# Convolution, spectral mixing and a gated output on one NeuronCore: unit borders, early transposes and the order around the last mixing

## Chip, cores and metric

One core of one Trainium2 chip runs the kernel; seven idle. The metric is the device time of one execution in microseconds (us), lower is better. Engines: TensorE (PE; its weight loads are shown as PEld), VectorE (DVE), ScalarE (ACT), GpSimd (POOL) and SyncE (SP). TensorE writes its results into PSUM, which has eight banks; DVE and ACT take them from there. POOL's queue issues all loads but one, SP's queue issues all stores.

## What is computed

x has shape (8, 3264, 192): batch, sequence, channels, float32. First a causal convolution of 7 taps along the sequence, one softmaxed set of taps for each of 8 heads of 24 channels. Its output u goes through a Fourier transform along the sequence of which the first 64 modes are kept; each mode has its own complex 192x192 matrix; the inverse transform y is added and a gated term follows.

```python
w = softmax(weight)                                # (8 heads, 7 taps)
x = einsum('hk,bskhg->bshg', w, x_unfolded)        # convolution
X = rfft(x, axis=1)[:, :64]
Y = X * (w_r + 1j * w_i)                           # per mode a 192x192 product
u = x + irfft(Y, n=S, axis=1)
return u + maximum(u @ w_ch, 0)
```

## The kernel before, in words

The order of all work is written out by hand: the program's order is each engine's order, and semaphores are set from what each instruction reads and writes.

**Layout.** Batches are taken in four pairs, q = 0 to 3. The sequence of a pair is cut into NB = 13 blocks of 256 positions; a block lies on 128 partitions with two positions each, so a pair has NT = 26 tiles of 128 rows by 2 batches by 192 channels. xall holds all 52 blocks in bf16; the convolution reads its input there and writes its result into the slots one block before. ct holds the transposed rows of all tiles, 312 pieces of 128x128; its last 108 pieces first hold weight groups 5 to 10. arena holds tables at first, then weight groups, at last the output buffers. The 64 modes are 16 groups of four (g); two DMAs bring a group (real and imaginary half), and group g+11 goes where group g was, once mixing g has read it.

**Convolution** (conv_pieces, conv_step; L286 to L345). The work is cut into units, each a run of n blocks of one pair: 5 and 8 blocks for pair 0, 7 and 6 for each of the others. A unit has 8 heads of two steps; a step is four matmuls of the lower 64 rows and, two steps later, four of the upper 64, into one PSUM bank (L297, 64x64 array tiles, 48 n columns). After a head, DVE and ACT copy its results to xall (L334 to L344). While a unit's loads (load_unit, L147, on POOL's queue) have not landed, its matmuls wait. At the head of the program L184 runs 85 idle matmuls, and L434 a few more behind unit 0.

**Transform** (dft, L352): per tile one matmul with ftab, the table of cosines and sines, all tiles of a pair summed in one bank in two or three runs; xtrans (L366) transposes the sums into xt, the input of the mixing. Both are put between heads of the next unit (loop at L438).

**Transposes** (c_bank, L400): eight tiles' pieces are transposed into a bank (L398) and copied to ct by DVE or ACT in turn (two to one). 39 such banks are needed before the output. One is done ahead of the last transform run (L470), the others stand in the list tjobs (L501) behind four banks that transpose ftab and one that makes wsw from w_ch (w_bank).

**Mixing** (L650 to L692). For each pair of groups: mix (L515) twice, ACT's copy of the result (mix_copy, L527), three jobs of tjobs, mix_trans (transposes of the mixed modes, copied to yet by DVE and ACT), three more jobs. The last groups are interleaved with the first output pieces (both, L569) and zw_pair (L594): the mixed modes times w_ch and times the identity, for pairs 1 to 3, into zwl; mixings 14 and 15 are not in these, and their modes enter later as "late rows": late_rows (L529) computes them for all batches and POOL issues 16 small DMAs into zwl. For pair 0, zw is computed after mixing 15 (L686 to L692).

**Output** (L700 to L776). A tile's result is c (transposed rows times w_ch, from ct), plus g (ftab times zw's w_ch half), clamped at zero by ACT (L640), plus y (ftab times zw's other half), then DVE adds u (L629) and SP stores two tiles at a time. Tiles 0 to 3 are begun by hand; the other 100 ("items") go through a ring of eight PSUM banks, with the two row halves of different items side by side (L716). Item 0's c, and the g of tiles 0 to 3, stand right behind zw (L748 to L755).

Of the kernel before, what the change touches and what calls it, by code (L numbers as in the profile page):

```python
# [20 lines left out]
def kernel(  # L21
# [25 lines left out]
    MAGIC = 12582912.0  # L47
    NIDLE = 85
    UNITS0 = ((0, 5), (5, 8))
    UNITS = ((0, 7), (7, 6))  # L50
    units = [(q, b0, n) for q in range(NQ) for b0, n in (UNITS if q else UNITS0)]

# [93 lines left out]

    def load_unit(q, b0, n):  # L147
        nf = min(n, NB - 1 - b0)
        s0 = NB * q + b0 + 1
        for i in range(2):  # L150
            off = ((2 * q + i) * S + 2 * P * b0) * D
            src = bass.AP(tensor=x.tensor, offset=x.offset + off, ap=[[2 * D, P], [2 * P * D, nf], [1, 2 * D]])
            nc.gpsimd.dma_start(out=xin[:, s0:s0 + nf, 2 * D * i:2 * D * (i + 1)], in_=src)  # L153
        if nf < n:
            off = (2 * q * S + 2 * P * (NB - 1)) * D
            src = bass.AP(tensor=x.tensor, offset=x.offset + off, ap=[[2 * D, PL], [S * D, 2], [1, 2 * D]])
            nc.gpsimd.dma_start(out=xin[0:PL, s0 + nf, :].rearrange("p (i c) -> p i c", i=2), in_=src)  # L157
# [106 lines left out]
    for k, u in enumerate(units[4:]):  # L264
        load_unit(*u)
        if k == 1:
            nc.gpsimd.dma_start(out=wm[:, 0:D], in_=moe_w_ch[0:P, :])
        if k == 2:
            nc.gpsimd.dma_start(out=w1[64:P, 0:D], in_=moe_w_ch[P:D, :])
# [16 lines left out]
    def conv_pieces(step, row):  # L286

        (q, b0, n, h, a), z, _ = step
        s0 = NB * q + b0 + 1
        r = slice(64 * row, 64 * row + 64)  # L290
# [13 lines left out]
    def conv_step(u):  # L304
# [3 lines left out]
        if u is not None:  # L308
            if u[0]:
                z = free.pop(0)  # L310
            else:
                z = flow[-2][0][2] if u[4] else free.pop(0)
            flow[-1] = [(u, z[:, u[4] if u[0] == 0 else 0, :], z), []]
            lower = conv_pieces(flow[-1][0], 0)
# [6 lines left out]
        if old is not None:  # L321
            turn(old[1][2:])
            for _ in upper:
                pass
        if old is None or old[0][0][4] == 0:
            return
        (q, b0, n, h, _), _, tile1 = old[0]
        s0 = NT * q + 2 * b0
        dst = xall[:, s0:s0 + 2 * n, :, GRP * h:GRP * h + GRP].rearrange("p (b a) i e -> p a b i e", a=2)
        tile0 = flow[-2 - CONVLAG][0][2]  # L330
        if q == 0:
            srcv = tile0[:, :, 0:2 * GRP * n].rearrange("p a (b i e) -> p a b i e", b=n, i=2)
            if h in ((0, 1, 2, 3, 4, 6) if b0 == 0 else (0, 1, 3, 5)):
                nc.scalar.copy(out=dst, in_=srcv)  # L334
            else:
                nc.vector.tensor_copy(out=dst, in_=srcv)  # L336
# [14 lines left out]

    def dft(q, t0, t1):  # L352

        z = free.pop(0)
        xp = z[:, 0, 0:2 * D]
        for t in range(t0, t1):
            k = PL if t >= NT - 2 else P
            nc.tensor.matmul(xp, ftab[0:k, t, :], xall[0:k, NT * q + t, :, :],  # L358
                             start=(t == t0), stop=(t == t1 - 1), skip_group_check=True)
        if t0 == 0:  # L360
            nc.scalar.copy(out=xacc, in_=xp)
        else:
            nc.vector.tensor_tensor(out=xs[q % 2][:, :, :].rearrange("p i d -> p (i d)"), in0=xp, in1=xacc, op=ALU.add)
        free.append(z)
# [56 lines left out]
    for step in range(4):  # L421
        table(step, *PA)
    chores = {(0, 0): [(PB, (0,))], (0, 5): [(PA, (4,))], (0, H): [(PA, (5,)), (PB, (1, 2, 3)), (PC, range(4))],
              (1, H): [(PC, (4, 5))]}

# [5 lines left out]
    def idle(n):  # L431
# [4 lines left out]
        free.append(z)  # L436

    for k, u in enumerate(units):  # L438
        for h in range(H):
            for a in range(2):  # L440
                conv_step((*u, h, a))
            tables(k, h)
            if k > 1 and h == (4 if k == 2 else 2):
                if pend:
                    xtrans(pend.pop(0))
                dfts()
        if k == 2:
            for g in range(NW + NL):
                load_w(g)
        if u[0]:  # L450
            todo.append((u[0], 2 * u[1], 2 * (u[1] + u[2])))
            continue
# [3 lines left out]
        if k == 0:  # L456
            idle(4)
            dft(0, *PA)
            for step in (4, 5):
                table(step, *PB)  # L460
            idle(3)
        else:

            ones = open_psum("left", (1, 1, 1, 1)) + open_psum("right", (1, 1, 1, 1))
            free[:] = [ones[2 * twos.index(z) + i] for z in free for i in range(2)]
            todo.append((0, PA[1], NT))
    flush()

    z = free.pop(0)
    c_bank(8, z[:, 0, :].bitcast(BF16))  # L470
    free.append(z)
    dfts()
# [28 lines left out]
    tjobs = [(g_bank, 8 * k, min(8, NT - 8 * k)) for k in range((NT + 7) // 8)] + [(w_bank,)]  # L501
    tjobs += [(c_bank, k) for k in range(0, 3 * NT * NQ, 8) if k != 8]

    def some(n):
        for _ in range(n):
            if tjobs:
                f, *a = tjobs.pop(0)
                f(*a)

    def mix(g, bank):  # L510
        yp = bank[:, D * (g % 2):D * (g % 2) + D]
        for j in range(3):
            for p4 in range(4):
                m = 4 * g + p4
                nc.tensor.matmul(yp[32 * p4:32 * p4 + 2 * B, :], xt[:, j, :, m],  # L515
                                 wts[g][:, p4, j, :], start=(j == 0), stop=(j == 2),
                                 tile_position=(0, 32 * p4), skip_group_check=True)
        load_w(g + NW + NL)

# [8 lines left out]

    def late_rows(bank):  # L529

        m0 = MODES - 8
        for t in range(2):
            nc.tensor.matmul(bank[:, 0:2 * D], yet[:, t, 2 * B * m0:2 * B * MODES], (wm, w1)[t][:, :], start=(t == 0), stop=(t == 1),
                             skip_group_check=True)
        nc.scalar.copy(out=ylate, in_=bank[:, 0:2 * D])  # L535
        for m in range(8):
# [4 lines left out]

    def mix_trans(d, g0, n):
        et = [z.bitcast(BF16)[:, 0:n * P].rearrange("p (g k) -> p g k", g=n) for z in ze]
        for t in range(2):
            for g in range(n):
                trans(et[t][:, g, :], ymix[:, 2 * d + g0 + g, 64 * t:64 * t + P])
        m0 = 8 * d + 4 * g0
        for t in range(2):
            dst = yet[:, t, 2 * B * m0:2 * B * (m0 + 4 * n)].rearrange("p (m k) -> p m k", k=2 * B)
# [44 lines left out]
    def zw_pair(q, bw, by):  # L594

        for t, bank in enumerate((bw, by)):
            for i in range(2):
                zw_mm(2 * q + i, bank[:, D * i:D * i + D], t)
        for t, bank in enumerate((bw, by)):
            dst, srcv = zwl[:, 2 * q - 2:2 * q, t, :], bank[:, 0:2 * D].rearrange("p (b d) -> p b d", b=2)  # L600
            if t == 0:
                nc.scalar.copy(out=dst, in_=srcv)
# [46 lines left out]

    some(2)  # L650
    xtrans(NQ - 1, ze)
    some(2)
    ND = NG // 2

    for d in range(ND - 2):
        mix(2 * d, zm[d % 2])
        mix(2 * d + 1, zm[d % 2])
        mix_copy(d, zm[d % 2], 0, 2)
        some(3)
        mix_trans(d, 0, 2)  # L660
        some(3)
    d = ND - 2
    mix(2 * d, zm[0])
    some(99)
    mix(2 * d + 1, zm[0])
    mix_copy(d, zm[0], 0, 2)
    sl = [z[:, 0, :] for z in open_psum("left", (1, 1, 1, 1))]
    place[0] = sl[0:2]
    both(0, 0, "c", begin=True)
    mix_trans(d, 0, 2)  # L670
    both(0, 1, "c")
    zw_pair(1, ze[0], ze[1])
    zw_pair(2, sl[2], sl[3])
    d = ND - 1
    mix(NG - 2, zm[1])
    mix_copy(d, zm[1], 0, 1)
    zw_pair(3, zm[0], sl[2])
    mix_trans(d, 0, 1)
    mix(NG - 1, zm[1])
    mix_copy(d, zm[1], 1, 1)  # L680

    place[1], ze = ze, sl[2:4]
    both(1, 0, "c", begin=True)
    mix_trans(d, 1, 1)
    both(1, 1, "c")
    for b in range(2):  # L686
        zw_mm(b, zm[b][:, 0:D], 0)
    for b in range(2):
        zw_mm(b, ze[1][:, D * b:D * b + D], 1)
    nc.vector.tensor_copy(out=zw[:, 0, 0, :], in_=zm[0][:, 0:D])  # L690
    nc.scalar.copy(out=zw[:, 0, 1, :], in_=zm[1][:, 0:D])
    nc.vector.tensor_copy(out=zw[:, 1, 0:2, :].rearrange("p b d -> p (b d)"), in_=ze[1][:, 0:2 * D])  # L692

    def whole(n, which):
        for a in range(2):
            full(n, which, a)


# [4 lines left out]
    K = len(items)  # L703
    ring = ze + zm[1:2] + place[0] + place[1] + zm[0:1]
    taken = [0]
# [19 lines left out]
    def take(k):  # L725
        bank[k] = next_of_ring()
        place.setdefault(items[k][0], []).append(bank[k])

    def upper_y(k):
        if 0 <= k < K - 2:  # L730
# [17 lines left out]
    for k in range(LAG):  # L748
        take(k)
        for j, p in enumerate(pieces(k, 0, "c")):  # L750
            product(k, 0, p, j == 0, False)
        whole(k, "g")
        clamp(place[k][0], False)
        clamp(place[k][1])
    late_rows(zm[0])  # L755
    for k in range(K + 4):
# [52 lines left out]
```

## Time and profile before

| | us |
|---|---|
| median of three runs | 172.9 (172.82 to 173.41) |
| the profiled execution | 173.26 |
| its span, first to last instruction | 171.5 |
| TensorE busy | 161.1 (94%) |
| DVE / ACT / POOL busy | 128.3 / 113.7 / 51.8 |
| convolution, L297 | 9.5 to 69 |
| mixings 0 to 15, L515 | 74.7 to 103.1 |
| output loop, L716 without a gap | 108.9 to 165.7 |

The granted TensorE clock was 0.997 on average. The page has a row for each engine with its busy tenths in 40 slices of 4.3 us, and one for the 16 DMA engines; the chain of waits goes back from the last instruction to what released each step; the list of waits gives for each pair of engines and lines the total, the number and the longest. In the timeline a row is start, duration, engine, line, operation, and in brackets the idle time before it with what ended it. Four steps of the order below (L297, L358, L398, L515) are the convolution, the transform, the transposes and the mixing.

### The profile page before, as it was taken

What the parts mean: (1) busy time and instruction counts of PE and PEld (TensorE: products, weight loads), DVE (VectorE), ACT (ScalarE), POOL (GpSimd) and SP (SyncE); (2) the same over time, 40 slices, a digit from 0 to 9 for tenths busy, and PEclk for the clock granted to TensorE, in tenths of its full rate; (3) what the DMA queues carried; (4) which work ended last, traced back from release to release, by engine and by line L of the source; (5) the groups of instructions that cost most, each with busy time, mean ns of one, the idle gap of its engine ahead of it and who ended that gap; (6) DMA issues with size and microseconds to landing.
All of it is one profiled execution on the core that took longest, in us unless ns stands there. A gap on an engine that the chain in (4) does not pass through costs nothing.

```text
span 171.5 us, 6925 instructions
## 1 busy us (share of the span) xinstructions
PE 161.1 (94%) x2897; PEld 134.8 (79%) x2897; DVE 128.3 (75%) x262; ACT 113.7 (66%) x226; POOL 51.8 (30%) x93
## 2 busy tenths in 40 slices
PE   6998989999998999979999999999999999999980
PEld 6984867877867687669999875699898989898950
DVE  4899964637747384567776846799998999999990
ACT  8485874546546274277777664688888888888870
POOL 7998432424322453444432000790000000000000
PEclk9999999999999999999999999999999999999998
DMA  2999999999999999999999950489999989999995
GB/s 30 202 203 204 204 208 198 204 203 202 205 202 205 210 204 207 207 206 207 206 206 207 206 90 4 147 303 351 340 330 344 345 320 352 345 333 336 334 360 193
DMA packets 37151, 40.14 MB, mean 234 GB/s; under 512 B 2464, under 2 KB 37120, under 8 KB 37120
## 3 DMA queue, kind: packets, MB, share of 16 engines
q0 software_dynamic: 22816, 19.62, 71.4%
q1 hardware_dynamic: 14304, 20.09, 31.9%
q8 instruction: 22, 0.36, 0.8%
q14 instruction: 9, 0.07, 0.1%
HBM read 39.10 MB, written 20.05 MB: 345 GB/s over the span
## 4 chain that ended last, share of the span: by engine, by line
PE 80%; DMA 10%; POOL 3%; ACT 2%; issue 1%; DVE 0%; POOLq 0%; ACTq 0%; DVEq 0%
PE z L716 34%; PE z L297 16%; PE z L398 12%; DMA xall<-in_x_dram 10%; PE z L358 10%; PE z L515 3%; POOL xall L153 3%; PE z L647 1%; PE z L591 1%; PE z L375 1%; PE z L592 1%; PE z L582 1%; ACT ftab L393 1%; ACT z L479 1%; POOL xall L157 0%
## 5 line engine op out<-in xcount | busy, mean ns | idle before, releaser
L629 DVE TENSOR_TENSOR arena<-z,xall 128x384 f32<-128x384 f32 (+1 forms) x103 | 56.4, 557 | 3.4 <-PE z L716 1.5
L640 ACT ACTIVATE z<-z 128x384 f32<-128x384 f32 x102 | 48.5, 475 | 12.2 <-PE z L716 2.4
L716 PEld LDWEIGHTS <-ct 64*128 64x128 bf16 x600 | 42.3, 94 | 3.7 <-PE z L647 0.6
L716 PE MATMUL z<-arena,ftab 64*128 64x384 bf16 x308 | 44.9, 322 | 0.0
L297 PE MATMUL z<-xall,shared 64*64 64x336 bf16 (+3 forms) x1024 | 38.6, 294 | 1.8 <-DMA xall<-in_x_dram 1.0
L297 PEld LDWEIGHTS <-shared 64*64 64x64 bf16 x1024 | 33.2, 106 | 7.4 <-issue 4.9
L716 PE MATMUL z<-wsw,ct 64*128 64x192 bf16 x300 | 35.1, 243 | 0.0
L344 DVE CAST xall<-z 128x336 bf16<-128x336 f32 (+1 forms) x48 | 22.9, 483 | 12.5 <-PE z L297 10.2
L716 PEld LDWEIGHTS <-ftab 64*128 64x128 bf16 x396 | 29.7, 93 | 2.7 <-issue 0.5
L342 ACT CAST xall<-z 128x336 bf16<-128x336 f32 (+1 forms) x48 | 20.1, 418 | 15.4 <-PE z L297 11.3
L716 PE MATMUL z<-wm,ct 64*128 64x192 bf16 x200 | 29.9, 243 | 0.0
L716 PE MATMUL z<-w,ct 64*128 64x192 bf16 x100 | 24.3, 243 | 0.0
L395 DVE COPY ct<-z 128x1024 bf16<-128x1024 bf16 x27 | 17.4, 686 | 5.5 <-PE z L398 2.4
L398 PE MATMUL z<-ident,xall 128*128 128x128 bf16 x312 | 19.8, 219 | 0.0
L358 PE MATMUL z<-xall,ftab 128*128 128x384 bf16 (+1 forms) x104 | 18.3, 327 | 0.7 <-DVE xall L336 0.7
L398 PEld LDWEIGHTS <-xall 128*128 128x128 bf16 x312 | 17.8, 98 | 1.0 <-issue 0.2
L153 POOL DMA_DIRECT2D xall<-in_x_dram x16 | 14.7, 930 | 9.9 <-DMA xall<-in_x_dram 9.1
L358 PEld LDWEIGHTS <-ftab 128*128 128x128 bf16 (+1 forms) x104 | 9.6, 98 | 8.0 <-issue 1.2
L716 PE MATMUL z<-mixa,ftab 64*128 64x384 bf16 x88 | 13.6, 323 | 0.0
L393 ACT COPY ct<-z 128x1024 bf16<-128x1024 bf16 x12 | 12.1, 1012 | 2.1 <-PE z L398 1.9
L539 POOL DMA_DIRECT2D arena<-xs x16 | 7.9, 504 | 16.6 <-ACT xs L535 16.6
L184 PE MATMUL z<-xall 128*128 128x144 bf16 x85 | 7.9, 276 | 1.6 <-DVE xall L171 1.6
(113 smaller groups left out, 155.0 us busy)
## 6 DMA issues: line engine op xcount, KB each, us to landing
out_dram<-arena SPq DMA_DIRECT2D x47, 384.0 KB, 3.4
xall<-in_x_dram POOLq DMA_DIRECT2D x8, 672.0 KB, 16.8
xall<-in_x_dram POOLq DMA_DIRECT2D x8, 480.0 KB, 16.8
arena<-in_moe_w_r_dram POOLq DMA_DIRECT2D x10, 288.0 KB, 11.1
arena<-in_moe_w_i_dram POOLq DMA_DIRECT2D x10, 288.0 KB, 11.2
ct<-in_moe_w_r_dram POOLq DMA_DIRECT2D x6, 288.0 KB, 11.4
ct<-in_moe_w_i_dram POOLq DMA_DIRECT2D x6, 288.0 KB, 11.5
out_dram<-arena SPq DMA_DIRECT2D x4, 288.0 KB, 3.2
```

Source lines behind the costliest of these rows:

```text
L153: nc.gpsimd.dma_start(out=xin[:, s0:s0 + nf, 2 * D * i:2 * D * (i + 1)], in_=src)
L184: nc.tensor.matmul(free[3][:, 0, 0:144], zeros[:, 0:P], zeros[:, 0:144], start=True, stop=True, skip_group_check=True)
L297: yield nc.tensor.matmul(o, band[r, h, int(a != a1), c0:c0 + 64], xin5[r, s1:s1 + n, :, a1, dsl], start=(row == 0 and a1 == 0), stop=(row ...
L342: nc.scalar.copy(out=dst[:, a], in_=srcv)
L344: nc.vector.tensor_copy(out=dst[:, a], in_=srcv)
L358: nc.tensor.matmul(xp, ftab[0:k, t, :], xall[0:k, NT * q + t, :, :], start=(t == t0), stop=(t == t1 - 1), skip_group_check=True)
L393: nc.scalar.copy(out=out, in_=in_)
L395: nc.vector.tensor_copy(out=out, in_=in_)
L398: nc.tensor.matmul(o, in_, ident[:], start=True, stop=True, is_transpose=True)
L629: nc.vector.tensor_tensor(out=o[0:pn, :, a, :], in0=srcv, in1=xall[0:pn, s + a, :, :], op=ALU.add)
L640: nc.scalar.activation(out=z, in_=z, func=ACT.Relu)
L716: mm = nc.tensor.matmul(target(bank[k], cols, r), l, r, start=first, stop=last, skip_group_check=True)
```

## The change

- Units are counted over all 52 blocks: 5, 8, 9, 10, 10, 10, so that three of them cross from one pair to the next (parts_of splits them for the loads and the transform). Six units instead of eight, 768 convolution matmuls instead of 1024.
- Pair 0's remaining transform (tiles 6 to 25) stands right behind unit 1 instead of inside unit 2; for its first ten tiles heads 0 to 5 come first, heads 6 and 7 after.
- Four banks of transposes (fill) stand ahead of unit 3, two ahead of unit 4; the one ahead of the last transform stays. The last banks of ct, where weights lie, are held back until those are mixed (clear). Behind the last transform, xtrans is followed by four jobs instead of two.
- c of ring item 0 moves ahead of mixing 15; the ring's banks get another order.
- late_rows is split: its matmuls (late_mm) stand ahead of the g of tiles 0 to 3, its copy and DMAs stay.
- One reader to a bank: zw of pair 0 goes into two banks, one copied by ACT, one by DVE (before: three); the last mix_trans uses one bank and one DVE copy; zw_pair computes 384 columns per batch in one bank instead of 192 columns four times in two.
- The sine table's step 4 of the last third moves from behind unit 1 to its head 5; the moe_w_ch loads move by one unit; idle matmuls 92 instead of 85 at the start, three fewer behind unit 0.

```diff
-    NIDLE = 85
-    UNITS0 = ((0, 5), (5, 8))
-    UNITS = ((0, 7), (7, 6))
-    units = [(q, b0, n) for q in range(NQ) for b0, n in (UNITS if q else UNITS0)]
+    NIDLE = 92
+    UNITS = (5, 8, 9, 10, 10, 10)
+    units = [(sum(UNITS[:k]), n) for k, n in enumerate(UNITS)]
...
+    def parts_of(g0, n):
+        while n > 0:
+            q, b0 = divmod(g0, NB)
+            m = min(n, NB - b0)
+            yield q, b0, m
+            g0, n = g0 + m, n - m
...
-    def dft(q, t0, t1):
+    def dft(q, t0, t1, early=0):
...
+        DE = 6 * GRP
+        work = [(t, slice(0, DE)) for t in range(t0, t0 + early)] + [(t, slice(DE, D)) for t in range(t0, t0 + early)]
+        work += [(t, slice(0, D)) for t in range(t0 + early, t1)]
...
+    def fill(n):
+        for _ in range(n):
+            z = free.pop(0)
+            c_bank(8 * next(early_banks), z[:, 0, :].bitcast(BF16))
+            free.append(z)
+    early_banks = iter(range(1, 9))
     for k, u in enumerate(units):
+        fill({3: 4, 4: 2}.get(k, 0))
...
-            if k > 1 and h == (4 if k == 2 else 2):
-                if pend:
+            if k > 1 and h in (2, 6):
+                if pend and (k, h) != (2, 2):
                     xtrans(pend.pop(0))
-                dfts()
+                if h == 2:
+                    dfts()
...
-            idle(3)
...
-            todo.append((0, PA[1], NT))
+            dft(0, PA[1], NT, 10)
+            pend.append(0)
...
-    tjobs += [(c_bank, k) for k in range(0, 3 * NT * NQ, 8) if k != 8]
+    tjobs += [(c_bank, k) for k in range(0, 3 * NT * NQ, 8) if not 8 <= k < 64]
+    def clear(f, a):
+        last = a[0] + 7 - (3 * NT * NQ - NL * WGB // P) if f is c_bank else -1
+        return last < 0 or NW + last // (WGB // P) < mixed[0]
...
     some(2)
     xtrans(NQ - 1, ze)
-    some(2)
+    some(4)
...
+    ring = [sl[3], zm[0], sl[2]] + sl[0:2] + ze + zm[1:2]
...
     mix_trans(d, 0, 1)
+    take(0)
+    lower_c(0)
     mix(NG - 1, zm[1])
     mix_copy(d, zm[1], 1, 1)
-    place[1], ze = ze, sl[2:4]
+    place[1] = ze
     both(1, 0, "c", begin=True)
-    mix_trans(d, 1, 1)
+    mix_trans(d, 1, 1, sl[2])
     both(1, 1, "c")
     for b in range(2):
-        zw_mm(b, zm[b][:, 0:D], 0)
+        zw_mm(b, zm[0][:, D * b:D * b + D], 0)
     for b in range(2):
-        zw_mm(b, ze[1][:, D * b:D * b + D], 1)
-    nc.vector.tensor_copy(out=zw[:, 0, 0, :], in_=zm[0][:, 0:D])
-    nc.scalar.copy(out=zw[:, 0, 1, :], in_=zm[1][:, 0:D])
-    nc.vector.tensor_copy(out=zw[:, 1, 0:2, :].rearrange("p b d -> p (b d)"), in_=ze[1][:, 0:2 * D])
+        zw_mm(b, sl[2][:, D * b:D * b + D], 1)
+    late_mm(zm[1])
+    nc.scalar.copy(out=zw[:, 0, 0:2, :].rearrange("p b d -> p (b d)"), in_=zm[0][:, 0:2 * D])
+    nc.vector.tensor_copy(out=zw[:, 1, 0:2, :].rearrange("p b d -> p (b d)"), in_=sl[2][:, 0:2 * D])
```

## The prediction

> **What bounds the kernel now.** I read the page first: busy shares and the 40 slices.
>
> ```profile
> PE 161.1 (94%) x2897; PEld 134.8 (79%) x2897; DVE 128.3 (75%) x262; ACT 113.7 (66%) x226; POOL 51.8 (30%) x93
> ...
> PE   6998989999998999979999999999999999999980
> ...
> DMA  2999999999999999999999950489999989999995
> ```
>
> Two things are full at once. TensorE is full from slice 6 on; the DMA engines are full from slice 1 to 22 (4 to 99 us) with loads alone, then empty for 9 us. So until about 100 us TensorE and the load stream run side by side, and only the later of them counts. The chain of waits in order of time shows which one the profile followed:
>
> ```profile
> 24.48 3.04 PE z L297 x72
> ...
> 68.96 0.55 PE z L398 x8
> ...
> 69.52 2.14 PE z L358 x12
> ...
> 102.73 0.42 PE z L515 x12
> ...
> 108.94 56.78 PE z L716 x936
> ```
>
> It is TensorE throughout. But how far behind is the stream? Its last issue, the second half of weight group 15, stands in the timeline, and the view of that line and moment gives its time to landing:
>
> ```profile
> 90.85 0.61 POOL L276 DMA_DIRECT2D arena<-in_moe_w_i_dram  x1 [0.56 <-DMA arena<-in_moe_w_i_dram]
> ...
> DMA to landing us min/median/max: 11.2/11.2/11.2
> ```
>
> 90.85 + 11.2 = 102.05 us. Mixing 15, the first to read it, starts at 102.66 in TensorE's timeline:
>
> ```profile
> 102.45 0.28 PE L398 MATMUL z<-ident,shared 128*128 128x128 bf16 x2
> 102.66 0.46 PE L515 MATMUL z<-arena,mixa 128*16 128x192 bf16 x12
> 103.43 0.26 PE L582 MATMUL z<-wm,ct 64*128 64x192 bf16 x2 [0.31 <-DVE yet L552]
> ```
>
> So whatever TensorE saves before mixing 15, only some 0.5 us can reach the end; the rest turns into a wait for weights. What is saved behind mixing 15 counts in full, because L716 then runs 57 us without a gap. TensorE's own waits ahead of it, from the list of waits:
>
> ```profile
> PE z L297 <- DMA xall<-in_x_dram: 1.0, 2, 0.7
> PE z L515 <- ACT mixa L386: 1.0, 1, 1.0
> PE z L297 <- issue: 0.9, 1, 0.9
> ```
>
> **The change, part by part. Load stream.** The same 20 x loads, the same 32 weight loads, the same bytes; borders move, and the two small moe_w_ch loads move by one unit. The stream ran at 198 to 210 GB/s in every slice, with issues of 480, 672, 144 and 288 KB alike, so 288 KB pieces (3 blocks) are priced as the rest: group 15 lands at 102.05 as before. Each POOL issue waits for the landing of the one eight before it; by the rate below the eight in flight never hold less than 6 us of transfers, so POOL's standing longer in unit 3's five issues, with the building of ident, perm and apart behind them, starves nothing. Those matrices are first used at 33 us. Unknown: about 508 fewer TensorE instructions need fewer instruction fetches (page, q8: 22 packets for 5794 instructions, so 2 fewer; 0.8% of 16 engines' span is 22 us, 1.0 each). Bounds: 0, and 2 us if both fell on the one DMA engine that lands last; I take 0, as 16 engines share them.
>
> **Convolution units.** 256 fewer matmuls and weight loads, each matmul longer. Is a matmul's time a floor or its columns? In three short windows, starts of L297 lie 30.5 ns apart for 6 blocks (60 from 38.2 to 40.0), 34.9 for 7 (44 from 25.7 to 27.2), 39.6 for 8 (49 from 19.0 to 20.9): 5 ns per block each time. Columns are unchanged, so the gain is 0; the chain's L297 after 24.3 stays 27.6 us for 39 blocks, 0.71 a block. Evictions: DVE 458 and 508 ns for 6 and 7 blocks, ACT 398 and 438, so 658 and 558 for 10, below the 800 ns of a 10-block head; hidden there, with banks of slack.
>
> **Rows.** Conv waited for rows with 13 blocks in until 17.67 and with 20 in until 24.48: 0.97 us a block. Units 2 to 5 (22, 32, 42, 52 blocks) then have rows at 26.4, 36.2, 46.1, 55.8 (0.2 for moe_w_ch). TensorE after: unit 1 ends at 23.78. Pair 0's remaining transform, 20 tiles in 3.36, now fills the 0.70 wait. Split in ten, 288 columns lie between rows of 83 ns (192 columns) and 171 (384), 96 columns at 58 (128) or below: 127 + 58 against 171, +0.14 for ten tiles, at worst +0.8. Its heads 6 and 7 come after 1.3 us of the others, about when DVE's last copy ended (25.03). Unit 2 from 27.3 (rows 26.4), 6.4 + 0.5 for xtrans: 34.2. Four transposed banks at 0.46 (52 transposes took 3.01): 36.1, rows 36.2. Unit 3 with 18 transform tiles at 0.171: 46.4. Two banks: 47.3, rows 46.1. Unit 4 with 20 tiles and xtrans: 58.3, rows 55.8. Unit 5 the same: 69.3. A bank, 20 tiles: **last transform at 73.2**, against 71.66 now, with six banks (2.8) more behind it. The 92 - 85 idle matmuls (0.4 us) and the removed three lie ahead of the wait that ends at 17.67: nothing.
>
> **Mixing stage.** Now last transform to mixing 15 takes 102.66 - 71.66 = 31.0. Off: seven banks (six, and bank 0 that goes into the 1.0 us wait for the mixa copy), 3.24, and w_bank 0.27; on: c of ring bank 0, 0.35 (row 105.25: three L716), and 0.25 because w_bank needs ACT's first ftab copy (ended 74.25) so that bank 0 overruns the gap. 28.1, so TensorE could start mixing 15 at 101.3. Group 15 is usable at 102.05 + 0.14 (lag seen from landing to matmul at 24.48) = **102.19: -0.47**. TensorE has 0.9 us to spare. Mixings 12 to 14 wait less than 1 us, their groups coming every 2.8 us.
>
> **Behind mixing 15** (before: 102.66 to 107.07, 4.41 us, no other gap than 0.31). c of item 0 is gone: -0.35. The 0.31 wait for DVE's yet copy goes, as that copy now lies ahead of the weights' wait; late next is ACT's mix copy (starts 0.52 after the mixing, 0.33, 0.06 more), 0.13 behind the six c matmuls: net -0.18. late_mm (0.42) moves ahead of g and lies beside the new zw copy: ACT takes 0.48 for 384 columns (row of L602) where DVE took 0.36 and ACT 0.32 side by side, from 0.59 after the first zw matmul, done 0.25 before late_mm ends; without that cover 0.5 would show. The single DVE copy of yet (0.21 for 128 columns) replaces 0.19 and 0.21 in parallel: 0. Behind the ACT copy queue two clamps, then the copy for the 16 late-row issues of POOL; before they landed 3 us ahead of pair 1's start, so nobody waits. Pairs 1 to 3: four 384-column matmuls at 0.163 (row 106.65) for eight at 0.083: 0. SP's queue is unchanged. Sum -0.53.
>
> **Total -1.0 us.** The profiled execution was 173.26 (span 171.5, 1.8 around it): 172.3. The median shown is 0.36 lower: **171.9**. The output loop keeps its instructions; DVE's 103 adds of 557 ns there leave 1.8 us of slack and shift with it.
>
> [...] Rows first: between 2 and 4 us 20 idle matmuls ran, between 7 and 9 us 36 of the same: TensorE started slow and sped up after some 5 us. The largest later gap, 1.0 us, slowed nothing. [...]
>
> **Rivals.** (1) *Only the stream's 0.5 us arrives*: the tail's waits change names (zw on one engine, late_mm ahead of g). For it: ACT's copy is 0.12 longer. Against: 0.25 us of cover. 172.4. (2) *Weights land sooner*, by the fetches: up to 0.9 us until TensorE's 101.3 binds, 171.0. (3) *TensorE late, slower than before*: the six banks do not fit in the waits. Their copies (DVE 0.69, ACT 1.01) stand in front of the heads' evictions and hold banks. It decides at the last transform: up to 74.1 the weights still hide it, from 75.1 the kernel is slower than before. If DVE's four fill copies (2.8 us) all stall TensorE, 76.0, mixing 15 at 104.1: +0.9, 173.8. For it: DVE is 80% used per head of 10 blocks. Against: eight banks rotate, two in flight. (4) *Clock falls* during a wait for weights: a ramp of 5 us at half rate costs 2.5: 174.4. Against: each wait below 1 us. That the change does nothing cannot be: the order of instructions changes as said.
>
> **Chances.** Forecast 0.70 (171.5 to 172.3: 0.3 either way for the landing, 0.2 for seams); (1) 0.12; (2) 0.05; (3) 0.10; (4) 0.03. 0.5% is 0.86 us, about what a measurement here can tell from no change; the forecast lies just beyond it, so its 0.70 splits into 0.51 faster and 0.19 within. Faster 0.51 + 0.05 = 0.56; same 0.19 + 0.12 + 0.01 of (3) = 0.32; slower 0.12. The range reaches from half of (2) to the slow side without the worst of (3): 171.3 to 172.9.
>
> **What would show it.** Right: mixing 15 waits for the DMA of group 15 (0.5 to 1 us) and starts near 102.2; the output loop starts 3.9 us later; L297 stays near 27.6 us in the chain; the 0.70, 0.86 and 1.0 waits are gone. Wrong: mixing 15 released by TensorE's own work, a landing of group 15 off 102 by over 0.4, a new gap between zw and g, or DVE as releaser in the convolution.

## The result and the profile after

The changed kernel takes **172.53 us** (median of 21 runs, 172.01 to 173.04) where the kernel before takes 173.09 (21 runs, 172.71 to 173.54): a ratio of 0.9967, 95% interval [0.9956, 0.9978]. That is 0.56 us faster, inside the 0.5% that the prediction counted as "same"; it had named 171.9. In the profiled executions of two kernels below (e5_front_80, e9_after_skip15) the granted clock fell to 0.50, for 6.8 and 3.4 us, so for these two the time is read from their other runs.

| us from the start of the span | before | after | difference |
|---|---|---|---|
| last transform ends | 71.66 | 73.45 | +1.8 |
| group 15 of the weights landed | 102.02 | 101.98 | -0.04 |
| mixing 15 starts | 102.66 | 102.03 | -0.63 |
| output loop on item 2 (its last c starts) | 108.10 | 106.88 | -1.22 |
| TensorE's last matmul ends | 166.82 | 165.59 | -1.23 |
| last store landed | 170.46 | 169.49 | -0.97 |
| span | 171.50 | 170.53 | -0.97 |
| the profiled execution's time | 173.26 | 172.53 | -0.73 |
| its time less its span | 1.76 | 2.00 | +0.24 |

The page of the changed kernel, busy shares, slices of TensorE and of the DMA engines:

```profile
PE 160.2 (94%) x2643; PEld 126.2 (74%) x2643; DVE 125.6 (74%) x245; ACT 110.2 (65%) x209; POOL 50.7 (30%) x93
...
PE   6996989999999999999999989999999999999980
...
DMA  2999999999999999999999960579999989999894
```

The picture is the old one, with 254 TensorE instruction pairs and 17 instructions each of DVE and ACT fewer. What has moved is seen in the chain of waits in order of time (start, duration, what; number of instructions):

```profile
34.51 1.89 PE z L411 x32
36.41 2.55 PE z L309 x46
...
56.44 10.11 DMA arena<-in_moe_w_i_dram
...
66.83 11.23 DMA ct<-in_moe_w_i_dram
...
78.35 12.14 DMA arena<-in_moe_w_i_dram
...
90.77 11.21 DMA arena<-in_moe_w_i_dram
102.03 0.48 PE z L543 x12
...
107.72 56.78 PE z L710 x936
```

From 56 to 102 us the chain now runs through the loads: 90.77 + 11.21 is the landing of group 15's second half, and mixing 15 follows 0.05 us later. Before, TensorE stood there instead. L710 is the output loop, 56.78 us as before, but 1.22 us sooner. TensorE's timeline around mixing 15 (in brackets: idle time ahead and what ended it) and its list of waits:

```profile
100.86 0.33 PE L710 MATMUL z<-wsw,ct 64*128 64x192 bf16 x2
102.03 0.46 PE L543 MATMUL z<-arena,mixa 128*16 128x192 bf16 x12 [0.85 <-DMA arena<-in_moe_w_i_dram]
```

```profile
PE z L543 <- DMA arena<-in_moe_w_i_dram: 0.8, 1, 0.8
PE z L309 <- issue: 0.4, 1, 0.4
PE z L309 <- DMA xall<-in_x_dram: 0.3, 1, 0.3
PE z L411 <- ACT shared L556: 0.2, 1, 0.2
```

TensorE was ready at 101.18 and waited 0.85 us. The old waits (1.0 for the mixa copy, 0.7 for rows, 0.31 for DVE's yet) are gone. The span became 0.97 us shorter where 1.0 was forecast, but that this agrees is partly luck: the loop gained 1.22, more than forecast, and the last landing took 0.26 of it back. Another 0.24 us was lost outside the span.

### The profile page after: what moved, and what is told of

Its sections match the earlier page's. It is cut to its first block, busy times and chain, and to the rows that moved or that the text cites. A ratio compares the mean times of both kernels' runs of the same rounds, so it can differ in the third digit from the quotient of the medians.

```text
span 170.5 us, 6352 instructions
## 1 busy us (share of the span) xinstructions
PE 160.2 (94%) x2643; PEld 126.2 (74%) x2643; DVE 125.6 (74%) x245; ACT 110.2 (65%) x209; POOL 50.7 (30%) x93
## 4 chain that ended last, share of the span: by engine, by line
PE 58%; DMA 33%; POOL 3%; issue 2%; ACT 1%; POOLq 0%; ACTq 0%
PE z L710 34%; DMA arena<-in_moe_w_i_dram 20%; PE z L309 14%; DMA xall<-in_x_dram 7%; DMA ct<-in_moe_w_i_dram 7%; PE z L370 6%; POOL xall L165 2%; PE z L411 2%; PE z L690 1%; POOL arena L288 0%; ACT xall L351 0%; PE z L631 0%; ACT z L683 0%; PE z L543 0%; ACT arena L670 0%
## 5 line engine op out<-in xcount | busy, mean ns | idle before, releaser
L710 PEld LDWEIGHTS <-ct 64*128 64x128 bf16 x600 | 42.3, 94 | 3.7 <-PE z L690 0.6
L710 PE MATMUL z<-arena,ftab 64*128 64x384 bf16 x308 | 44.9, 322 | 0.0
L309 PE MATMUL z<-xall,shared 64*64 64x480 bf16 (+3 forms) x768 | 38.8, 338 | 0.8 <-issue 0.4
L710 PE MATMUL z<-wsw,ct 64*128 64x192 bf16 x300 | 35.1, 243 | 0.0
L309 PEld LDWEIGHTS <-shared 64*64 64x64 bf16 x768 | 25.0, 106 | 12.2 <-issue 1.9
L710 PEld LDWEIGHTS <-ftab 64*128 64x128 bf16 x396 | 29.7, 93 | 2.7 <-issue 0.5
L353 DVE CAST xall<-z 128x480 bf16<-128x480 f32 (+1 forms) x32 | 20.6, 645 | 12.7 <-PE z L309 11.8
L710 PE MATMUL z<-wm,ct 64*128 64x192 bf16 x200 | 29.9, 243 | 0.0
L351 ACT CAST xall<-z 128x480 bf16<-128x480 f32 (+1 forms) x32 | 17.5, 548 | 14.9 <-PE z L309 14.9
L710 PE MATMUL z<-w,ct 64*128 64x192 bf16 x100 | 24.3, 243 | 0.0
L408 DVE COPY ct<-z 128x1024 bf16<-128x1024 bf16 x27 | 18.4, 688 | 5.2 <-PE z L411 2.9
L370 PE MATMUL z<-xall,ftab 128*128 128x384 bf16 (+3 forms) x114 | 18.0, 312 | 0.2 <-DVE xall L353 0.2
L370 PEld LDWEIGHTS <-ftab 128*128 128x128 bf16 (+1 forms) x114 | 10.2, 98 | 7.6 <-issue 1.5
L710 PE MATMUL z<-mixa,ftab 64*128 64x384 bf16 x88 | 13.6, 323 | 0.0
L288 POOL DMA_DIRECT2D arena<-in_moe_w_r_dram x10 | 6.1, 614 | 11.2 <-PE z L411 4.5
```

Source lines behind the costliest of these rows:

```text
L309: yield nc.tensor.matmul(o, band[r, h, int(a != a1), c0:c0 + 64], xin5[r, s1:s1 + n, :, a1, dsl], start=(row == 0 and a1 == 0), stop=(row ...
L351: nc.scalar.copy(out=dst[:, a], in_=srcv)
L353: nc.vector.tensor_copy(out=dst[:, a], in_=srcv)
L370: nc.tensor.matmul(xp[:, :, ds], ftab[0:k, t, :], xall[0:k, NT * q + t, :, ds], start=(j == 0), stop=(j == len(work) - 1), skip_group_chec ...
L408: nc.vector.tensor_copy(out=out, in_=in_)
L710: mm = nc.tensor.matmul(target(bank[k], cols, r), l, r, start=first, stop=last, skip_group_check=True)
```

## Experiments

Theory: the weight stream gates mixing 15, the rest of the gain lies behind it, and what is missing sits after TensorE's last matmul: in the stores, and outside the span. Rivals: one half of the change does harm; another wait took the old ones' place; TensorE's convolution costs more than its columns.

### Both kernels once more

No edit; the kernel before and the changed one, one profile each.

> The kernel before, unchanged, profiled once more. Forecast's theory (TensorE is 0.6 us later than the weights at mixing 15): the 0.86 us stall of TensorE at 55 us is there again, mixing 15 starts 0.5 to 0.7 us after group 15 has landed, span 171.5. Rival (the stall belonged to that one execution, in most executions the kernel before waits for the weights too): no stall, mixing 15 within 0.2 us of the landing near 102.2, span about 171.0.

> The changed kernel, unchanged, profiled once more. Both theories: mixing 15 waits 0.5 to 1.0 us for group 15, starts 0.05 to 0.15 us after its landing, loop starts 3.6 us after it. A landing that differs from 101.98 by more than 0.2 us would show that the time of the changed kernel spreads with the load stream.

Before: 172.62 us, span 170.83. Its wait at 55 us was 0.44 us instead of 0.86 (in the list of waits, the row below), and with nothing behind it to absorb the difference, mixing 15 came at 102.18 instead of 102.66:

```profile
PE z L297 <- issue: 0.4, 1, 0.4
```

```profile
101.98 0.28 PE L398 MATMUL z<-ident,shared 128*128 128x128 bf16 x2
102.18 0.46 PE L515 MATMUL z<-arena,mixa 128*16 128x192 bf16 x12
102.96 0.26 PE L582 MATMUL z<-wm,ct 64*128 64x192 bf16 x2 [0.31 <-DVE yet L552]
```

Group 15 landed at 102.05 here, so TensorE came only 0.13 us behind the weights: this is nearer to the rival than to the forecast's theory, though TensorE's own work still released mixing 15.

After: 172.31, span 170.28. Mixing 15 waited 0.80 us and started at 102.13, 0.05 us after the landing, as expected; the loop stood at 106.98. In this pair the loop gains 0.64 us, the span 0.55. So the profiled execution before, on which the sum was made, was a late one: its span of 171.5 lies 0.2 above the median of the runs, and the trace of the tail alone (below), which has the old front, shows a wait of 0.44 us at 55 us too. While the weights decide when mixing 15 starts, such a delay of TensorE is not passed on. The changed kernel has delays of its own, though: its 21 runs lie 1.03 us apart, those of the kernel before 0.83. What makes the wait at 55 us (its releaser is "issue") vary was not tried.

### Each half alone

```diff
 # tail alone, the core
+    take(0)
+    lower_c(0)
     mix(NG - 1, zm[1])
...
-    late_rows(zm[0])
+    late_rows(zm[1])
 # front alone, the core
-    UNITS = ((0, 7), (7, 6))
+    UNITS = (5, 8, 9, 10, 10, 10)
...
+        fill({3: 4, 4: 2}.get(k, 0))
```

Tail alone: the edits behind the transform (late_mm, mix_trans with a bank, zw_pair, take(0) and lower_c(0) ahead of mixing 15, the ring's order), with the old units and job list. Front alone: units, fill, the split transform, clear, four jobs behind xtrans, with the old order behind.

> Units, transform, fills and job list as before; c of ring bank 0 ahead of mixing 15, late_mm ahead of g, one reader to a bank as in the changed kernel. Forecast's theory: about half of the gain, -0.5 of the 1.0 us in the trace, and mixing 15 itself a little later (0.35 us of c put in front of it, TensorE being last there), so the time -0.2 to -0.5 us. Rival (before waits for weights anyway): the whole measured gain, -0.5 to -0.6 us.

> Units, early transform, fills, job list as in the changed kernel; everything behind mixing 14 as before. Forecast's theory: mixing 15 starts at 102.1 to 102.2 instead of 102.66, time -0.5 us. Rival (before waits for weights anyway): 0.0, within 0.15 us. If the loop's start moves by 0.5 and the time does not, the stores at the end give it back.

Tail alone: 172.71 us against 173.16, ratio 0.9977 [0.9958, 0.9996]. Mixing 15 started at 102.59 without a wait, c of item 0 ahead of it; the loop's first c of item 2 at 107.44. Behind mixing 15 it takes 4.85 us where the kernel before takes 5.44 in both its traces: -0.59. But c of item 0 only moved to the other side, as nothing there waits: ahead of mixing 15 it costs TensorE time again (102.59 against 102.18 in the trace before with the same wait at 55 us). The gain of 0.45 us lies in the forecast's range and 0.05 short of the rival's, so it does not tell the two apart.

Front alone: **174.37**, ratio 1.0086 [1.0066, 1.0106], slower than before, where forecast and rival had expected -0.5 and 0.0. Yet mixing 15 came at 102.02, and TensorE's last matmul ended at 166.36, 0.46 earlier than in the first trace before and as in the second (166.34). Its last stores were slow. The landing times of the stores issued from 163.8 us on, before and then front alone:

```profile
DMA to landing us min/median/max: 3.1/3.1/3.4
```

```profile
DMA to landing us min/median/max: 3.8/4.1/4.4
```

What else happened then? Queue q8 moves instructions in fetches of 16 KB: 22 packets with 0.36 MB before, and 20 in the changed kernel, whose TensorE has 254 instruction pairs fewer; that they are TensorE's is what the two runs of the next section show. In the output loop one comes every 6.7 to 8.1 us. In the traces before and after, from the loop's second fetch on, a store issued 0.8 to 1.9 us ahead of a fetch, so that it is in flight when the fetch comes, takes 0.3 to 1.9 us longer than the one before it (after: 4.7 against 2.8 us, ahead of the fetch at 157.3), and each store behind it some 0.2 us less (4.5, 4.3, 4.1, 3.9 us). Before, the last fetch is at 158.7; front alone has 21 of them, the last at 165.6. The page's rows, before and then front alone:

```profile
q8 instruction: 22, 0.36, 0.8%
```

```profile
q8 instruction: 21, 0.34, 0.8%
```

### Moving that fetch

The number of idle matmuls at the head sets how many instructions TensorE has ahead of the end; they lie in a wait for rows.

```diff
 # front alone, 12 matmuls and 12 weight loads fewer
-    NIDLE = 92
+    NIDLE = 80
 # the changed kernel, 12 and 12 more
-    NIDLE = 92
+    NIDLE = 104
```

> The front part alone with 80 idle matmuls at the start in place of 92, so 24 TensorE rows fewer (5288, as many as the changed kernel); the idle matmuls lie in a wait for rows in both. Theory of the instruction fetch: the front part alone lost 1.2 us against the kernel before because its TensorE needed a 21st fetch of 16 KB, at 165.6 us, in the last 0.3 us of its work, and the last stores then took 3.8 to 4.4 us to land instead of 3.1 to 3.4. With 24 rows fewer there is no 21st fetch; the last stores land 3.2 to 3.5 us after their issue, and the time falls by 0.8 to 1.2 us against the front part alone, to 173.1 to 173.5. Rival, the order of work behind mixing 15 is what made the front part slow: the time stays at 174.2 to 174.5.

> The changed kernel with 104 idle matmuls at the start in place of 92 (24 TensorE rows more, 5312); the twelve matmuls lie ahead of the wait for rows that ends near 17.4 us. Theory of the instruction fetch: a 21st fetch appears within the last microsecond of TensorE's work, the last stores land 4.2 to 4.7 us after their issue instead of 3.4, and the kernel takes 0.8 to 1.2 us more than the changed kernel, 173.3 to 173.7, so that it is slower than the kernel before. Rival, fetches and stores have nothing to do with each other: 172.4 to 172.7, as the changed kernel.

Front alone with 80: 173.17 us (11 runs), ratio 1.0015 [1.0002, 1.0029]: 1.20 us less than with 92. The changed kernel with 104: 173.22 (12 runs), ratio 1.0020 [0.9999, 1.0041]: the gain is gone. Three of the twelve took 174.3 to 174.5 at the same clock as the others (0.992 to 0.995; the others 0.989 to 0.997); no trace shows why. TensorE's last matmul ended at 165.65, as in the changed kernel (165.59); a fetch at 164.3 had come in, and the stores behind it landed late, the last at 170.22 instead of 169.49. The landing times of its stores issued from 163.8 us on, and then those of the changed kernel:

```profile
DMA to landing us min/median/max: 3.9/4.0/4.2
```

```profile
DMA to landing us min/median/max: 3.3/3.4/3.4
```

The first expectation held. Of the second, fetch and slow stores came, but in smaller sizes: landings of 3.9 to 4.2 us where 4.2 to 4.7 were expected, and 0.69 us of time where 0.8 to 1.2 were. Both rivals fell. That fetch and stores meet on a DMA engine is argued from these times; no run shows the engine.

### The time outside the span

In the kernel before it is 1.79 us (median of 29 runs, 1.74 to 1.84), in the tail alone 1.78; in the changed kernel 1.97 (1.81 to 2.14), in the front alone 2.19. With the units, DVE and ACT lost instructions, and an 8 KB fetch (queue q14) that lay at 162.2 us now lies at 172.3, behind the span's end. The page's rows, before and after:

```profile
q14 instruction: 9, 0.07, 0.1%
```

```profile
q14 instruction: 8, 0.07, 0.1%
```

So 32 tiny instructions were put into units 2 to 5, on both engines, on ACT alone, on DVE alone:

```diff
             tables(k, h)
+            if k > 1:
+                nc.vector.memset(pad[:, 0:2], 0.0)
+                nc.scalar.copy(out=pad[:, 32:34], in_=halfpi[:, 0:1].to_broadcast([P, 2]))
```

> The changed kernel with 32 tiny instructions more on ScalarE and 32 more on VectorE, one pair in each head of units 2 to 5 (they write a scratch tile that nobody reads), so that both have as many instructions ahead of their last ones as in the kernel before. Theory: the time outside the span rose from 1.77 to 1.98 us because one of these engines' 8 KB instruction fetches, at 162.2 us in the kernel before, slid to 172.3 us, behind the last landing, where the program's end waits for it; with the padding it comes back to 162 us, the time outside the span to 1.77 us, and the kernel takes 172.3 us, 0.2 less than the changed one. Rival, the time outside the span has another cause: 1.98 us stay, 172.5. Should the pads delay the evictions, TensorE's work would slip by less than 0.9 us into the wait for weights and the loop would not see it.

> The changed kernel with the 32 tiny instructions on ScalarE alone. The padding on both engines brought the 8 KB fetch back from 172.3 to 161.2 us, the time outside the span to 1.78 us and the kernel to 172.27 us. If that fetch is ScalarE's: fetch at 161 to 162 us, 1.78 us outside the span, 172.3 us. Rival, it is VectorE's: fetch at 172 us, 1.97 us outside, 172.5 us.

> The changed kernel with the 32 tiny instructions on VectorE alone; on ScalarE alone they changed nothing (172.74 us, 1.98 us outside the span, a fetch at 172.9 us). If the late 8 KB fetch is VectorE's: the last fetch at 161 to 163 us, 1.78 us outside the span, 172.2 to 172.4 us. Rival, it takes both engines' padding: fetch near 172 us, 1.98 us outside, 172.5 to 172.7 us.

| | last q14 fetch | outside the span | time | ratio to before |
|---|---|---|---|---|
| changed kernel | 172.3 | 1.97 | 172.53 | 0.9967 [0.9956, 0.9978] |
| both padded | 161.2 | 1.78 | 172.27 | 0.9945 [0.9926, 0.9964] |
| ACT alone | 172.9 | 1.98 | 172.74 | 0.9984 [0.9972, 0.9997] |
| DVE alone | 160.9 | 1.78 | 172.28 | 0.9967 [0.9952, 0.9982] |

The fetch is VectorE's, and it is worth 0.2 us outside the span: with 32 more instructions on VectorE 1.78 us lie there instead of 1.97. This is read from the time outside the span, as the median span is 170.5 us in the changed kernel and in both kernels with VectorE padded. The medians of the time alone would not show it: the kernel before moves between 172.90 and 173.16 from one set of runs to the next, and beside its own 172.90 the kernel with VectorE padded has the same ratio as the changed one. One more trace agrees: the profiled execution of e9_after_skip15 (below) has no such fetch behind its span, and its time outside is 1.76. The rivals of the first and the third expectation fell, and so did the thought that the fetch could be ScalarE's. The front alone has 2.19 us outside, and 2.17 with 80 idle matmuls, for which this fetch (at 173.6 us there) does not account in full; that stays open.

### Does the weight stream gate mixing 15?

```diff
     def load_w(g):
-        if g < NG:
+        if g < NG - 1:
```

Group 15 is not loaded; mixing 15 uses what lies there.

> The changed kernel without the two loads of weight group 15; mixing 15 reads the weights of group 4, which lie in the same place. Theory of the prediction, the load stream sets the start of mixing 15 and TensorE is ready 0.85 us sooner: mixing 15 starts at 101.2 to 101.4 without a gap ahead of it, the output loop 0.7 to 0.85 us sooner, and the time falls by as much, to 171.7 to 171.9. Rival, another wait is hidden behind the one for the weights (a bank, a copy of the mixing stage): mixing 15 stays at 101.8 or later and the time at 172.3 to 172.5.

> The changed kernel without the two loads of weight group 15 once more, for an undisturbed trace: in the profiled execution before, the granted clock was 0.5 from 17.9 to 21.3 us and TensorE came 1.6 us late. The timed runs gave 172.05 us, 0.48 less than the changed kernel, where 0.7 to 0.85 was expected. If the wait for weights alone held mixing 15 (0.85 us in the trace of the changed kernel): mixing 15 at 101.2 to 101.5, output loop 0.5 to 0.8 us sooner, and what the time does not show is lost between the loop's start and the last landing. If TensorE's own work holds it: mixing 15 at 101.6 or later.

The timed runs: 172.03 us without the profiled one (172.05 with it), ratio 0.9943 [0.9924, 0.9961]. In the first profile the clock was at half for 3.4 us early on (below), which made TensorE late (mixing 15 at 102.41). The second, 171.70 us, is clean:

```profile
100.95 0.33 PE L710 MATMUL z<-wsw,ct 64*128 64x192 bf16 x2
101.20 0.46 PE L543 MATMUL z<-arena,mixa 128*16 128x192 bf16 x12
```

No wait, mixing 15 at 101.20, the loop 0.83 us sooner, the last landing 0.72. So TensorE's own time is 101.2 and nothing else hides behind the weights. The median moved only 0.50, less than the 0.7 to 0.85 expected; what the other runs lost was not seen in a trace.

### The transposes in the waits, and the units

```diff
 # without the six early banks (they return to the job list)
-        fill({3: 4, 4: 2}.get(k, 0))
+        fill(0)
 # units of 7 and 6 again
-    UNITS = (5, 8, 9, 10, 10, 10)
+    UNITS = (5, 8, 7, 6, 7, 6, 7, 6)
```

> The changed kernel without the six banks of transposes in front of units 3 and 4; they go back into the mixing stage's list of jobs, at 0.46 us each. Theory of the prediction: the banks lay partly in waits for rows, so that the last transform comes at most 1.8 us sooner, and the mixing stage grows by 2.8 us; TensorE, which was 0.85 us ahead of the weights at mixing 15, reaches it 0.2 to 1.5 us behind them: mixing 15 at 102.2 to 103.5, released by TensorE's own work, and the time 172.7 to 174.0 (my point: 173.0). Rival, rows are never what TensorE waits for in these units: the transform comes 2.8 us sooner, mixing 15 still waits for its weights, and the time is 172.5.

> The changed kernel with units of 7 and 6 blocks again for pairs 1 to 3 (six units in place of four; 256 matmuls and 256 weight loads more, 16 evictions more on each of VectorE and ScalarE, the same columns); the six banks of transposes stand at the starts of pairs 2 and 3. 5800 TensorE rows, 512 more, so the last fetch stays where it was. Theory of the prediction, a convolution matmul costs its columns and nothing else: the last transform ends at 73.0 to 73.7, mixing 15 still waits for its weights, and the time is 172.3 to 172.6. Rival, each matmul carries a cost of its own of 5 to 10 ns: the last transform ends 1.3 to 2.6 us later, at 74.6 to 75.9, the wait for weights is gone and the time grows by 0.4 to 1.7 us, to 172.9 to 174.2.

Without the banks: 172.67 us, ratio 0.9978 [0.9964, 0.9991]. TensorE waited for rows instead, and its last transform ended 1.50 us sooner (71.95); the mixing stage took 2.5 us more. Mixing 15 came at 102.19, now by TensorE's own work:

```profile
PE z L309 <- DMA xall<-in_x_dram: 1.9, 2, 1.5
```

```profile
101.94 0.32 PE L710 MATMUL z<-wsw,ct 64*128 64x192 bf16 x2
102.19 0.46 PE L543 MATMUL z<-arena,mixa 128*16 128x192 bf16 x12
```

So the six banks save TensorE 1.0 us (102.19 against 101.18), of which the weights let 0.16 through: they are nearly free to leave out. This is the theory's side, at its lower edge: 102.2 and 172.7 were the least it expected, and the point of 173.0 was too high.

With units of 7 and 6: 172.72 us, ratio 0.9979 [0.9964, 0.9995]. The last transform ended at 74.01, 0.56 later: 0.31 beyond the theory's bound and 0.59 short of the rival's. The traces bound the size. Added from each matmul's start to the next one's, waits left out, the convolution behind unit 1 takes 27.76 us here, 27.27 in the changed kernel and 27.53 in the kernel before. So 256 matmuls more, with the same columns, cost 0.26 to 0.49 us, an estimate of 1 to 2 ns each: not nothing, but far from the rival's 5 to 10. It does not matter here, as mixing 15 still waited 0.80 us for its weights; in this trace these landed at 102.48, 0.3 to 0.6 us later than in all the others that loaded them. Whether that belongs to the units or to the execution is open. The smaller units also gave VectorE its instructions back: its last fetch lies at 163.0 us, and the time outside the span is 1.79.

## Why the prediction was wrong, point by point

- **Last transform at 73.2, TensorE ready at 101.3, group 15 at 102.05**: 73.45, 101.18 and 101.98. The rows, the split transform and the jobs were priced nearly rightly: the transform came 0.25 us late, and the stage behind it took 27.7 us instead of 28.1. The second trace without group 15 confirms the 101.2. That the units gain 0 was off by 0.26 us (27.53 to 27.27), which the wait for weights hides.
- **Mixing 15: -0.47.** In the profiled pair -0.63: landing 0.07 sooner, and 0.05 us from landing to matmul where 0.14 was taken. In the other pair of traces only -0.05, since there the kernel before started it at 102.18. The term was sized on one execution, and a late one.
- **Behind mixing 15: -0.53.** -0.59 in the two traces of the changed kernel and in the tail alone. No wait took the place of DVE's; the cover for ACT's zw copy held, with 0.15 us instead of 0.25 (copy done at 104.59, late_mm at 104.74).
- **"DVE's 103 adds ... shift with it"**: the loop and TensorE's end did shift, by 1.22 and 1.23 us. The last landing moved by 0.97: the last store, issued at 166.1 instead of 167.4, took 3.4 us instead of 3.1. In the second pair it took 3.0 against 2.9, and the landing lost only 0.09, so this part differs from execution to execution. The fetches of instructions, which the prediction weighed only for the loads (2 fewer, taken as 0, and 0 it was: group 15 landed at 101.98 instead of 102.02), delayed stores here: 3.9 to 4.2 us to landing with a fetch at 164.3, 3.3 to 3.4 without it.
- **The failed step: "The profiled execution was 173.26 (span 171.5, 1.8 around it): 172.3. The median shown is 0.36 lower: 171.9."** Both parts took something as fixed that is not. The time around the span grew by 0.2 us, because VectorE's last fetch slid past the end, from 162.2 to 172.3 us; the padding shows it. The sum had nothing for this term and gave no reason. And the 0.36 did not carry over: the changed kernel's median equals its profiled execution. Of it, 0.19 was the median of three runs (172.9; over 21 runs 173.09), and 0.17 the profiled execution's own lateness. That a kernel that waits for weights does not have this lateness is argued from the two pairs of traces, not tested by an edit. The miss of 0.63 is 0.20 (outside the span, 2.00 where 1.8 was taken) + 0.03 (span, 170.53 where 170.5 was forecast) + 0.36 + 0.04 of rounding. As a change: of the forecast -1.0 us, the median spans show about -0.8, since the term for mixing 15 was taken from a late execution, and +0.2 outside the span leaves the measured -0.56.
- **Rivals.** The time comes near that of (1), 172.4, but not by its mechanism: both halves arrived, and the end gave some back. (2) fell: the landing did not move. (3) fell: the banks stalled nothing. (4) did not happen in the two traces of the changed kernel, with mean clocks of 0.997 and 0.998. In its other runs the mean clock, 0.98 or more, does not exclude a fall, as the first trace without group 15 has 0.98 too and did show one; it happened there (0.50 for 3.4 us) and in one execution of the front alone with 80 (0.50 for 6.8 us), see below. The 5 us at half rate were the author's estimate from the idle matmuls at the start; the runs showed these 3.4 and 6.8 us.

In spans, over all runs, the change is worth about 0.8 us (171.3 to 170.5, medians): the tail alone 0.45 (171.4 to 170.95), the front with 80 idle matmuls, that is without TensorE's late fetch, 0.3 (171.3 to 171.0).

## What to carry to other kernels

A forecast that ends at the last matmul is not done: follow it through the last landing and the end of the program. Here 12 matmuls and 12 weight loads more on TensorE, in a wait, brought a fetch at 164.3 us and 0.69 us of time, and 32 tiny instructions on VectorE moved one from 172.3 to 160.9 us, worth 0.2. When a change removes instructions, look in the profile where the last fetches of TensorE and of the other engines lie, and where they will lie. And ask of the profiled execution how it stands among many runs, and whether its lateness is one that the changed kernel would still pass on: here a term of 0.47 us was 0.63 in one pair of traces and 0.05 in the other.

## What was not expected of the hardware

- **A fetch of TensorE's instructions in its last 1.3 us costs 0.7 to 1.2 us here** (changed kernel with 104 against 92: 173.22 and 172.53 us; front alone with 92 against 80: 174.37 and 173.17), by way of the stores that are still to land (3.9 to 4.2 us against 3.3 to 3.4 in the changed kernel); VectorE's 8 KB fetch behind the end costs 0.2 (1.97 us outside the span, 1.78 with VectorE padded).
- **The granted clock fell to half after stretches with 1.4 and 1.9 us of waiting.** In one execution of the front alone with 80 (176.09 us, 2.9 over the median of the others) and in the first trace without group 15, stretches of 3.41 us that held one wait were followed by a granted clock of 0.50, for 6.8 and 3.4 us. Columns: window, TensorE busy (instructions), granted clock, DMA share, GB/s. First the one, then the other:

```profile
97.20:100.64 3.44, 3.33 (x48) 1.00 1.04 175
100.64:104.05 3.41, 2.04 (x35) 1.00 0.08 14
104.05:107.47 3.42, 3.42 (x17) 0.50 0.03 7
107.47:110.88 3.41, 3.41 (x16) 0.50 0.03 7
110.88:114.30 3.42, 3.42 (x60) 1.00 0.69 234
```

```profile
14.44:17.85 3.41, 1.55 (x11) 1.00 1.31 203
17.85:21.27 3.42, 3.42 (x31) 0.50 1.32 204
```

TensorE was idle for 1.37 and 1.86 us of the stretch ahead; the longest waits in it were 1.29 us, for weights, and 1.86 us, put down to "issue". In the front alone with 92, 1.74 us in one stretch (from 14.1 us) and 1.23 in another (from 99.4) changed nothing, and in the changed kernel neither did 1.26 us (12.37 to 15.78 us; granted clock 1.00 in the next). What tells the stretches apart is open, and no edit tested whether the waits are the cause. Until that is known, a wait for weights of 1.3 us can't be called safe from it.
